# A transformer block on one core: value weights loaded from ScalarE's DMA queue, and the five engine queues rewritten

## The chip, the cores and the metric

The kernel runs on one core of a Trainium2 chip. The metric is the device time of one execution in microseconds (us), the median of several runs. A core has five engines with a queue of instructions each: TensorE (PE in the profile, its weight loads PEld), VectorE (DVE), ScalarE (ACT), GpSimd (POOL) and SyncE (SP), which here only issues DMAs. The DMAs of all queues move their bytes on the core's 16 DMA engines.

## The reference

One block, with x of 2048 rows and D = 448 columns, bf16, 16 heads of Dh = 28 and F = 1792:

```python
def _A_ref(x, wqkv, w_phi, wo):
    qkv = (x @ wqkv).reshape(B, S, 3, H, Dh)            # q, k, v
    pq, pk = einsum("bhsd,hdf->bhsf", q, w_phi), einsum("bhsd,hdf->bhsf", k, w_phi)
    phi_q = concat([softmax(pq), softmax(-pq)]);  phi_k = concat([softmax(pk), softmax(-pk)])
    kv = einsum("bhsf,bhsd->bhfd", phi_k, v);  z = einsum("bhsf->bhf", phi_k)
    num = einsum("bhqf,bhfd->bhqd", phi_q, kv)
    den = einsum("bhqf,bhf->bhq", phi_q, z)[..., None] + 1e-6
    return (num / den) @ wo
def _B_ref(x, w_gate, w_up, w_down):
    return (sigmoid(x @ w_gate) * (x @ w_up)) @ w_down
h  = x + _A_ref(layernorm(x), wqkv, w_phi, wo)
h2 = h + _B_ref(layernorm(h), w_gate, w_up, w_down)
```

Since kv sums over all 2048 rows, no query row can be finished before the last key row has been added.

## The kernel before

The rows are cut into 16 tiles t of 128. Names carry the tile: `pva7` belongs to tile 7. Work runs in stages.

**Head.** SP's queue loads x (`x0`, `x1` are one tile each, `x2`, `x4`, ... two tiles each) and the key and value weights (`ld_k0`, `ld_k2`, `ld_v0`, `ld_v2`), and ACT's queue loads the four small pieces of w_phi (`wphi0` to `wphi3`). Key weights are transposed on PE (`wT0` to `wT3`), copied out of PSUM (`wTe`), multiplied with w_phi (`w2m0_0` to `w2m0_3`) and copied out again (`w2e0_0` to `w2e0_3`): from then on a key projection gives pk directly. Per tile, DVE takes row statistics of x (`bst`, `agg`), POOL or DVE makes the reciprocal root (`ve1`, `pow1`, `nm1`, `nb1`), and one of three engines normalises (`xn`). Tiles 0 to 3 are transposed on PE (`xT`) and copied out (`xTe`); later tiles are transposed by a DMA that SP issues. PE fills its early waits with matmuls on zeros (`warm0`, ...).

**Key/value stage.** Tiles 0 to 3 are projected in pairs of tiles: `ppa`/`ppb` for pk, `vva`/`vvb` for v; later tiles one by one, `pva`/`pvb` doing both. Each a or b part is 8 or 6 matmuls on 64 rows of the array, an upper and a lower half side by side. ACT takes two exponentials of pk (`ek`), DVE sums them by head (`ss`) and inverts the sums (`rs`), POOL or DVE multiplies (`phi`), an engine copies v (`v1`), and PE adds the tile's share of kv (`kva`, `kvb`). The query weights are folded with w_phi in the same way (`ld_q`, `w2m1`, `w2e1`).

**Transition.** The query side (`pqa`, `pqb`, then `eq` on ACT) starts, the sums of kv are masked (`kvz`), and per tile come `num`, the division on DVE (`rsm`, `qq`, `b`, `c`, `den`, `rden`), `o` on POOL or DVE, a transpose (`oT`), the output projection (`woa`, `wob`), the residual (`h`), the second layernorm (`nm`, `sq`, `ve`, `pow2`, `hn`) and its transpose (`hT`).

**Second half.** `ga`, `gb` are gate and up for a group of tiles, `sig` (ACT) and `hh` (DVE) their product; `dn`, `dp`, `dm` the down projection, `fin` the last addition and `out` the store. The `dm` parts use all 128 rows of the array, the others 64 rows.

The program is a graph of such named operations. Their dependencies (and with them the semaphore waits) follow from the tiles that they read and write, but the order in which each engine runs them is written out by hand in `ORDER`, one list of names per engine; where an operation may run on two or three engines, the list that names it decides. An engine runs its list strictly in order, so an operation that waits holds up all that stand behind it. Lines that the prediction names: loads L388, copies out of PSUM L471, statistics L485 and L486, normalisation L511 and L514, paired matmuls L289, fillers L464, `ek` L599 and L600, `ss` L603, `rs` L604, `phi` L607, full-height matmuls L814.

Of the kernel before, what the change touches and what calls it, by code (L numbers as in the profile page):

```python
# [18 lines left out]
class Graph:  # L19
# [86 lines left out]
    def emit(self, nc):  # L106
# [114 lines left out]
    "pe": (
        "warm0 wT1 wT0 warm1 xT1 warm2 xT0 warm3 wT2 wT3 w2m0_0 warm4 w2m0_1 w2m0_3 w2m0_2 warm5 xT2 warm6 ppa0 warm7 "
        "ppb0 xT3 vva0 vvb0 ppa2 ppb2 vva2 vvb2 kva0 w2m1_1 w2m1_0 kvb0 kva1 pva4 kvb1 pvb4 w2m1_3 w2m1_2 pva5 pva6 "
        "pvb5 pvb6 kva2 pqa0_0 kvb2 pva7 kva3 pvb7 pva8 kvb3 pvb8 pva9 kva4 pvb9 kvb4 pva10 kva5 pvb10 pva11 kvb5 "
        "kva6 pvb11 kvb6 pva12 kva7 pvb12 pva13 kvb7 pvb13 kva8 pva14 kvb8 kva9 pvb14 kvb9 pqb0_0 kva10 pva15 kvb10 "
        "kva11 pvb15 kvb11 kva12 pqa0_1 kvb12 kva13 pqb0_1 kvb13 kva14 pqa1_0 kvb14 kva15 kvb15 pqb1_0 pqa1_1 num0 "
        "num1 pqb1_1 pqa2_0 pqb2_0 num2 pqa2_1 oT0 pqb2_1 oT1 num3 woa0 wob0 pqa3_0 num4 pqb3_0 pqa3_1 pqb3_1 num5 "
        "hT0 hT1 ga0_1 gb0_1 ga0_0 num6 gb0_0 ga0_3 woa2 gb0_3 ga0_2 wob2 gb0_2 num7 ga0_5 gb0_5 ga0_4 gb0_4 ga0_7 "
        "gb0_7 ga0_6 num8 gb0_6 woa4 ga0_9 ga0_8 gb0_9 gb0_8 wob4 ga0_11 ga0_10 gb0_11 gb0_10 woa6 num9 wob6 ga0_13 "
        "ga0_12 gb0_13 gb0_12 dn0_0 dn0_4 ga2_0 ga2_1 gb2_0 gb2_1 dn0_8 dn0_11 ga2_3 num10 ga2_2 gb2_3 dp0_0 gb2_2 "  # L230
        "dp0_4 ga2_5 ga2_4 gb2_5 gb2_4 dp0_8 dp0_11 ga2_6 ga2_7 gb2_6 gb2_7 woa8 ga2_8 ga2_9 gb2_8 gb2_9 wob8 num11 "
        "ga2_10 ga2_11 gb2_10 gb2_11 dn2_0 ga2_12 ga2_13 gb2_12 gb2_13 dn2_4 dn2_8 ga4_1 num12 gb4_1 ga4_0 dn2_11 "
        "gb4_0 dp2_0 ga4_3 ga4_2 gb4_3 dp2_4 num13 gb4_2 ga4_5 dp2_8 gb4_5 ga4_4 dp2_11 gb4_4 ga4_7 num14 gb4_7 ga4_6 "
        "woa10 gb4_6 ga4_9 wob10 gb4_9 ga4_8 num15 gb4_8 ga4_11 woa12 gb4_11 ga4_10 wob12 gb4_10 ga4_13 dn4_0 ga4_12 "
        "gb4_13 gb4_12 dn4_4 ga8_1 ga8_0 gb8_1 gb8_0 dn4_8 dn4_11 ga8_3 ga8_2 dp4_0 gb8_2 dp4_4 dp4_8 gb8_3 ga8_4 "
        "dp4_11 gb8_4 ga8_5 woa14 gb8_5 ga8_6 wob14 gb8_6 ga8_7 dn6_0 gb8_7 dn6_4 ga8_8 ga8_9 dn6_8 gb8_9 gb8_8 "
        "dn10_0 dn6_11 ga8_11 ga8_10 gb8_11 gb8_10 dp6_0 dp6_4 dp6_8 ga8_13 ga8_12 gb8_13 gb8_12 dp6_11 dn10_4 dn10_8 "
        "ga12_0 ga12_1 gb12_0 dn8_0 dn10_11 gb12_1 ga12_2 dp10_0 ga12_3 dn8_4 gb12_3 gb12_2 dp10_4 dn8_8 ga12_5 "
        "dn8_11 ga12_4 gb12_5 gb12_4 dp8_0 dp8_4 ga12_7 ga12_6 gb12_7 dp10_8 dp10_11 gb12_6 dp8_8 dp8_11 ga12_9 "
        "ga12_8 gb12_9 gb12_8 dm14_0 dm12_0 dm15_0 ga12_11 ga12_10 gb12_11 gb12_10 dm12_4 dm14_4 dm13_0 ga12_12 "  # L240
        "ga12_13 gb12_12 gb12_13 dm15_4 dm14_8 dm15_8 dm12_8 dm15_10 dm14_10 dm14_12 dm14_13 dm15_12 dm12_10 dm12_12 "
        "dm15_13 dm12_13 dm13_4 dm13_8 dm13_10 dm13_12 dm13_13 "
    ),
# [62 lines left out]
def build(nc, A_x, A_wqkv, A_w_phi, A_wo, B_w_gate, B_w_up, B_w_down, out):  # L306
# [10 lines left out]
    with ExitStack() as es:  # L317
# [570 lines left out]
```

The softmax here doesn't subtract the row's maximum and nothing guards it: scores larger than these inputs give would overflow.

## Time and profile before

| | |
|---|---|
| Median of 8 runs | 208.28 us (208.02 to 208.48) |
| The profiled execution | 208.14 us, span of its instructions 206.4 us |
| PE busy | 198.5 us (96%), 2457 matmuls |
| DVE, ACT, POOL busy | 136.6 (66%), 95.2 (46%), 58.9 us (29%) |
| DMA | 16.25 MB, of these 15.86 MB on queue q1 (SP) and 0.03 MB on q10 (ACT) |
| Chain that ended last | PE 87%, DVE 4%, POOL 3%, DMA 2% |

Busy time is the union of the instructions' spans. PE's matmuls are pipelined and overlap, so a busy PE may still lose time between two starts; how far apart the starts of consecutive operations lie says more. The profiled execution is 1.74 us longer than its span, and 0.14 us below the median.

### The profile page before, as it was taken

The page shows a single profiled execution, that of the slowest core. Times are in us where ns is not written, and L with a number is a line of the kernel's source. Part 1 is how long each engine was busy: PE and PEld are TensorE (multiplying, and loading weights), DVE is VectorE, ACT ScalarE, POOL GpSimd, SP SyncE. Part 2 cuts the span into 40 slices and gives each one's busy share as a digit, 9 for nine tenths or more (in the row PEclk, how much of TensorE's full clock was granted, in tenths as well). Part 3 has the DMA queues.
Part 4 walks back from the last instruction along what each step waited for, and adds up shares of the span by engine and source line. Part 5 has one row for each costly group of instructions (what it writes and reads, how often), then busy time and mean ns, then how long its engine had stood idle before and what let it go on. Part 6 is the DMA issues. An engine that isn't in the chain of part 4 may idle for free.

```text
span 206.4 us, 5794 instructions
## 1 busy us (share of the span) xinstructions
PE 198.5 (96%) x2457; PEld 111.6 (54%) x2457; DVE 136.6 (66%) x343; ACT 95.2 (46%) x185; POOL 58.9 (29%) x99
## 2 busy tenths in 40 slices
PE   7899999999989999999999999999999999999991
PEld 2736666775446666676444444445555545544450
DVE  5999999978899896767768977346332513353151
ACT  2699999879792536222333442334323122122100
POOL 4868999832345404400032020001400000000000
PEclk9999999999999999999999999999999999999999
DMA  6955444899022270414006511130521000020013
GB/s 162 277 117 141 79 93 89 249 380 283 31 51 54 54 183 6 79 29 51 3 0 79 121 29 25 21 35 22 56 71 25 3 0 3 0 89 3 0 38 118
DMA packets 32722, 16.25 MB, mean 79 GB/s; under 512 B 24952, under 2 KB 31800, under 8 KB 32696
## 3 DMA queue, kind: packets, MB, share of 16 engines
q1 hardware_dynamic: 32192, 15.86, 32.5%
q8 instruction: 19, 0.31, 0.7%
q10 hardware_dynamic: 504, 0.03, 0.2%
q14 instruction: 7, 0.06, 0.1%
HBM read 8.34 MB, written 1.84 MB: 49 GB/s over the span
## 4 chain that ended last, share of the span: by engine, by line
PE 87%; DVE 4%; POOL 3%; DMA 2%; issue 1%; ACT 1%; SPq 1%
PE psum L289 80%; PE psum L814 5%; DMA x_sb<-in_A_x_dram 2%; POOL o_pad L700 1%; PE psum L478 1%; POOL rst L728 1%; SPq L388 1%; DVE hn_pad L732 1%; DVE st L485 1%; ACT eq L637 0%; PE psum L553 0%; ACT eq L638 0%; POOL xn_pad L514 0%; PE psum L464 0%; DVE hhT L788 0%
## 5 line engine op out<-in xcount | busy, mean ns | idle before, releaser
L289 PE MATMUL psum<-xnT,wg_sb 64*128 64x512 bf16 (+1 forms) x490 | 94.6, 334 | 0.7 <-DVE qq L685 0.6
L289 PE MATMUL psum<-xnT,wu_sb 64*128 64x512 bf16 (+1 forms) x490 | 94.5, 334 | 0.3
L787 ACT ACTIVATE sg_sb<-psum 128x512 bf16<-128x512 f32 (+1 forms) x70 | 35.0, 511 | 89.9 <-PE psum L289 89.4
L788 DVE SCALAR_TENSOR_TENSOR hhT<-sg_sb,psum 128x512 bf16<-128x512 bf16 (+1 forms) x70 | 39.1, 575 | 50.8 <-ACT sg_sb L787 50.3
L289 PEld LDWEIGHTS psum<-xnT,wg_sb 64*128 64x128 bf16 x490 | 43.9, 94 | 23.9 <-DVE hhT L788 4.8
L289 PEld LDWEIGHTS psum<-xnT,wu_sb 64*128 64x128 bf16 x490 | 43.8, 94 | 15.2 <-PE psum L289 1.4
L289 PE MATMUL psum<-wd_sb,hhT 64*128 64x448 bf16 x336 | 37.1, 349 | 0.0
L289 PEld LDWEIGHTS psum<-wd_sb,hhT 64*128 64x128 bf16 x336 | 17.0, 94 | 15.0 <-DVE x_sb L718 0.6
L607 POOL TENSOR_TENSOR phi<-hhT,rs 128x896 bf16<-128x896 bf16 x13 | 22.7, 1767 | 2.6 <-DVE rs L604 1.5
L289 PE MATMUL psum<-wv_sb,xnT 64*128 64x448 bf16 x112 | 22.0, 350 | 0.1
L289 PE MATMUL psum<-Wk,xnT 64*128 64x448 bf16 x112 | 22.0, 350 | 0.1
L726 POOL TENSOR_SCALAR ve<-ssq 128x1 f32<-128x1 f32 x16 | 3.0, 190 | 61.2 <-ACT junk L723 60.5
L603 DVE TENSOR_REDUCE ss<-hhT 128x32 f32<-128x896 bf16 x16 | 17.0, 1070 | 1.1 <-ACT hhT L600 1.0
L700 POOL TENSOR_TENSOR o_pad<-c_sb,rden 128x448 bf16<-128x448 bf16 x12 | 11.2, 935 | 19.0 <-DVE rden L695 17.4
L289 PE MATMUL psum<-xnT,Wq 64*120 64x512 bf16 x112 | 14.7, 381 | 0.2
L289 PE MATMUL psum<-wo_e,oT 64*128 64x448 bf16 x56 | 13.2, 350 | 0.2 <-DVE oT L471 0.2
L289 PE MATMUL psum<-wo_o,oT 64*128 64x448 bf16 x56 | 13.2, 350 | 0.1
L289 PEld LDWEIGHTS psum<-v,phi 64*120 64x120 bf16 x256 | 10.9, 131 | 3.3 <-PE psum L289 0.2
L821 DVE SCALAR_TENSOR_TENSOR x_sb<-psum,x_sb 128x448 bf16<-128x448 f32 x16 | 9.4, 620 | 3.5 <-PE psum L814 3.1
L723 ACT ACTIVATE junk<-x_sb,nm 128x448 bf16<-128x448 bf16 x16 | 10.6, 663 | 2.2 <-DVE nm L721 2.1
L289 PE MATMUL psum<-v,phi 64*120 64x116 bf16 x256 | 11.1, 213 | 0.1
L814 PE MATMUL psum<-wd_sb,hhT 128*128 128x448 bf16 x56 | 11.1, 353 | 0.0
(82 smaller groups left out, 238.5 us busy)
## 6 DMA issues: line engine op xcount, KB each, us to landing
out_dram<-x_sb SPq DMA_DIRECT2D x16, 112.0 KB, 1.8
x_sb<-in_A_x_dram SPq DMA_DIRECT2D x7, 224.0 KB, 4.2
wd_sb<-in_B_w_down_dram SPq DMA_DIRECT2D x7, 224.0 KB, 3.9
wg_sb<-in_B_w_gate_dram SPq DMA_DIRECT2D x3, 448.0 KB, 6.2
wu_sb<-in_B_w_up_dram SPq DMA_DIRECT2D x3, 448.0 KB, 8.2
wv_sb<-in_A_wqkv_dram SPq DMA_DIRECT2D x2, 224.0 KB, 5.0
wk_sb<-in_A_wqkv_dram SPq DMA_DIRECT2D x2, 196.0 KB, 3.4
wo_e<-in_A_wo_dram SPq DMA_DIRECT2D x1, 336.0 KB, 3.3
```

Of the source, the lines that this page charges most:

```text
L289: p = e.matmul(o, lhsT=w, rhs=r, start=st, stop=sp, tile_position=(row, 0))
L388: return op(eng, name, lambda e: e.dma_start(dst, src), r=r, w=w, dma="in" if eng == "sp" else "ain", nring=48 if eng == "sp" else 8, kb=kb)
L478: p = e.transpose(ps[:, kt * P:(kt + 1) * P], src, ident[:])
L603: op("dve", "ss%d" % t, lambda e: e.tensor_reduce(ss[:, s, :], eks, AX.X, ALU.add), r=[("ek", s)], w=[("ss", s)])
L607: return e.tensor_tensor(phi[:, sp, :, :, :].rearrange("p a g (f n) -> p (a g f) n", f=2)[:, :, 0:56].rearrange("p b (h d) -> p b h d", h= ...
L700: return e.tensor_tensor(o_pad[:, so, off:off + D].rearrange("p (h d) -> p h d", h=H), c_sb[:, s, :, 0:DH], rden[:, s, :][:, :, None].to_b ...
L723: op("act", "sq%d" % t, lambda e: e.activation(junk[:, t % 2, :], h_sb[:, t, :], ACT.Square, bias=nm2[:, t:t + 1], accum_out=ssq2[:, t:t + ...
L726: op("pool", "ve%d" % t, lambda e: e.tensor_scalar(ve2[:, t:t + 1], ssq2[:, t:t + 1], 1.0 / D, EPS, op0=ALU.mult, op1=ALU.add), r=[("ssq2" ...
L787: op("act", "sig" + nm, lambda e: e.activation(sg_sb[:, k, 0:N], bk(bg)[:, 0:N], ACT.Tanh, scale=0.5), r=[B(bg)], w=[("sg", k)])
L788: op("dve", "hh" + nm, lambda e: e.scalar_tensor_tensor(out=hhT[(t0 // 4) % NHH][:, ff, ns], in0=sg_sb[:, k, 0:N], scalar=1.0, in1=bk(bu)[ ...
L814: p = e.matmul(bk(b)[:, 0:D], lhsT=hb[:, ff, TS(t)], rhs=wd_sb[:, ff, :], start=ff == 0, stop=ff == FT - 1)
L821: op("dve", "fin%d" % t, lambda e: e.scalar_tensor_tensor(out=h_sb[:, t, :], in0=bk(b)[:, 0:D], scalar=0.5, in1=h_sb[:, t, :], op0=ALU.mul ...
```

## The change

The two value loads are issued by ACT, behind the w_phi loads; key loads and x stay with SP. The fillers shrink from 9 of 512 columns and 36 of 128 columns to 9 and 16. All five lists in `ORDER` are written anew. In the head, x is loaded as x2, x0, then k2, x1, k0; DVE also normalises tile 0 and copies `w2e0_0`, ACT takes `wTe2`, `xT1e` and `xn2`; the value projection of tiles 0 and 1 starts before the key projection, and its parts alternate with those of the key projection. In the key/value stage some copies and `phi` change engines. Towards the transition, `pqb0_0` moves up beside `pqa0_0`; several weight loads change places. At the end, all `ga12`/`gb12` parts stand before the first `dm` part.

```diff
 ORDER = {
     "sp": (
-        "x1 x0 ld_k0 x2 ld_k2 x4 x6 ld_v0 x10 ld_v2 ld_q2 x8 ld_q3 ld_q1 ld_q0 xT4 xT5 xT6 x14 x12 xT7 ld_woe1 xT8 "
+        "x2 x0 ld_k2 x1 ld_k0 x4 x8 x6 x10 ld_q2 x14 ld_q3 ld_q1 ld_q0 xT4 xT5 xT6 x12 xT7 xT8 xT9 ld_woo1 xT10 xT11 "
+        "ld_wg2 xT12 ld_wd0 xT13 xT14 xT15 ld_wu0 ld_wu3 ld_wd5 ld_wg3 ld_wg1 ld_woe1 ld_wg0 ld_woe0 ld_wu1 ld_wd6 "
+        "ld_woo0 ld_wu2 ld_wd3 ld_wd2 oT3 oT2 ld_wd4 oT5 oT4 oT6 ld_wd1 oT7 hT2 hT3 oT8 oT9 hT5 hT4 hT6 hT7 oT10 oT11 "
...
     "act": (
-        "wphi3 wphi2 wphi1 wphi0 wTe1 wTe0 wTe3 w2e0_0 w2e0_1 w2e0_2 w2e0_3 xn3 xn4 ek0 ek1 xn5 v1_0 v1_1 xn6 ek2 ek3 "
+        "wphi0 wphi1 wphi3 wphi2 ld_v2 ld_v0 wTe2 wTe3 wTe1 wTe0 w2e0_2 xT1e w2e0_1 w2e0_3 xn2 xn3 v1_0 ek0 ek1 xn6 "
+        "ek2 v1_2 v1_3 ek3 w2e1_0 w2e1_1 ek4 v1_4 w2e1_2 w2e1_3 ek5 v1_5 xn10 v1_6 ek6 xn11 ek7 xn12 ek8 v1_8 xn13 "
+        "ek9 v1_9 xn14 ek10 xn15 ek11 ek12 v1_12 ek13 eq0_0 ek14 ek15 v1_15 v1_14 eq0_1 eq1_0 eq1_1 oT0e eq2_1 eq2_0 "
...
     "pe": (
-        "warm0 wT1 wT0 warm1 xT1 warm2 xT0 warm3 wT2 wT3 w2m0_0 warm4 w2m0_1 w2m0_3 w2m0_2 warm5 xT2 warm6 ppa0 warm7 "
-        "ppb0 xT3 vva0 vvb0 ppa2 ppb2 vva2 vvb2 kva0 w2m1_1 w2m1_0 kvb0 kva1 pva4 kvb1 pvb4 w2m1_3 w2m1_2 pva5 pva6 "
+        "warm0 wT2 wT3 warm1 wT1 wT0 warm2 xT0 warm3 w2m0_2 warm4 xT1 w2m0_1 w2m0_3 w2m0_0 warm5 vva0 ppa0 vvb0 ppb0 "
+        "xT3 xT2 vva2 ppa2 ppb2 w2m1_0 vvb2 kva0 w2m1_1 kvb0 pva4 kva1 pvb4 kvb1 pva5 w2m1_2 w2m1_3 pvb5 pva6 pqa0_0 "
...
     "dve": (
-        "zero bd0 bst1 agg1 bst0 agg0 ve1_0 nm1_0 nm1_1 xn1 bst2 bst3 agg2 agg3 ve1_3 xT0e wTe2 bst5 nm1_3 bst4 agg5 "
-        "agg4 bst6 xT1e ve1_4 bst7 agg7 agg6 bst10 xT2e bst11 agg10 xT3e nm1_6 ss0 agg11 rs0 ss1 bst8 rs1 bst9 agg8 "
+        "zero bd0 bst2 bst0 bst3 agg0 agg3 ve1_0 bst1 nm1_0 agg1 ve1_1 xn0 agg2 bst5 xn1 ve1_3 bst4 xT0e agg5 bst8 "
+        "agg4 w2e0_0 bst6 bst7 agg8 bst10 v1_1 agg7 agg6 ve1_6 xT3e xT2e ss0 rs0 ss1 agg10 rs1 bst11 bst9 ss2 agg9 "
...
     "pool": (
-        "ident0 phipad wqpad mask0 neghalf ident ve1_1 pow1_1 pow1_0 xn0 v1ones mask1 nm1_2 ve1_2 pow1_2 nb1_2 xn2 "
+        "phipad mask0 neghalf ident0 ident pow1_0 v1ones nm1_1 pow1_1 nm1_2 ve1_2 pow1_2 pow1_3 mask1 nm1_3 ve1_4 "
...
         def kload(a, b):
             load("ld_k%d" % a, wk_sb[:, a:b, :], A_wqkv[a * GP:b * GP, D:2 * D].rearrange("(kt p) n -> p kt n", p=GP),
-                 [("wk", kt) for kt in range(a, b)], (b - a) * 98)
+                 [("wk", kt) for kt in range(a, b)], (b - a) * 98, eng='sp')
 
         def vload(k):
             r0 = ROW0[k]
             load("ld_v%d" % k, wv_sb[:, k:k + 2, :], A_wqkv[r0:r0 + 256, 2 * D:3 * D].rearrange("(kt p) n -> p kt n", p=P),
-                 [("wv", k), ("wv", k + 1)], 224)
+                 [("wv", k), ("wv", k + 1)], 224, eng='act')
...
-        for i, (n, size) in enumerate(((9, 512), (1, 128), (5, 128), (1, 128), (8, 128), (9, 128), (9, 128), (3, 128))):
+        for i, (n, size) in enumerate(((9, 512), (5, 128), (2, 128), (1, 128), (4, 128), (4, 128))):
             op("pe", "warm%d" % i, warm(n, size), r=["zero"], w=[B(3)])
```

## The prediction

> **What bounds the kernel now.** I read the page first, then the busy time by stretches, the chain of waits, and in the timeline the few instructions on which the head hangs.
>
> ```profile
> PE 198.5 (96%) x2457; PEld 111.6 (54%) x2457; DVE 136.6 (66%) x343; ACT 95.2 (46%) x185; POOL 58.9 (29%) x99
> ```
>
> PE looks like the only bound. The stretches show where others stand beside it (columns: PE, PEld, DVE, ACT, POOL busy us, granted clock, DMA share, GB/s):
>
> ```profile
> 8.00:10.00 2.00, 1.81 (x33) 1.64 (x33) 2.00 (x8) 1.55 (x4) 1.73 (x5) 1.00 1.14 226
> 10.00:12.00 2.00, 2.00 (x23) 0.78 (x20) 1.97 (x8) 1.48 (x2) 1.77 (x8) 1.00 0.99 236
> 20.00:30.00 10.00, 10.00 (x144) 6.20 (x142) 9.96 (x23) 9.57 (x20) 9.62 (x13) 1.00 0.49 99
> 30.00:40.00 10.00, 10.00 (x170) 6.95 (x166) 9.45 (x15) 8.93 (x19) 9.44 (x6) 1.00 0.57 137
> ```
>
> Until 12 us the DMA engines are full and DVE has no gap. From 20 to 40 us all four compute engines are full: DVE is as much the bound of the key/value stage as PE. The chain shows the way in:
>
> ```profile
> 2.17 3.46 DMA x_sb<-in_A_x_dram
> ...
> 8.53 0.78 POOL xn_pad L514
> 9.31 0.05 issue
> 9.36 0.40 PE psum L478 x4
> 9.75 0.50 PE psum L464 x9
> 10.26 0.86 PE psum L289 x8
> ```
>
> Landing of x2, its normalisation, xT2, nine fillers, then the first projection ppa0. From there PE runs almost without holes. In the timeline, the first `ek` and the first and last links of DVE's stage (start, duration):
>
> ```profile
> 12.11 0.54 ACT L599 ACTIVATE hhT<-psum 128x448 bf16<-128x448 f32 x1
> 13.12 1.09 DVE L603 TENSOR_REDUCE ss<-hhT 128x32 f32<-128x896 bf16 x1 [0.19 <-ACT hhT L600]
> ...
> 43.76 1.09 DVE L607 TENSOR_TENSOR phi<-hhT,rs 128x896 bf16<-128x896 bf16 x1
> ```
>
> ss0 starts at 13.12, phi15 ends at 44.85, kva15 starts at 44.94: that is the stage, 31.7 us on DVE. The end of the chain:
>
> ```profile
> 184.83 2.38 PE psum L814 x12
> 187.20 3.13 PE psum L289 x28
> 190.33 2.38 PE psum L814 x12
> 192.71 3.13 PE psum L289 x28
> 195.84 6.17 PE psum L814 x32
> ```
>
> PE changes five times between 64-row and full-height parts.
>
> **The loads.** Landings in the trace, in order of issue: x1 2.86, x0 3.35, k0 4.78, x2 5.62, k2 6.43, x4 7.75, x6 8.36, v0 9.02, x10 9.58, v2 10.23. That is 112, 224, 420, 644, 840, 1064, 1288, 1512, 1736, 1960 KB in sum. Each load lands some 4 to 5 us after issue, though SP issues one in 0.47 us: bytes set the pace, not issuing. So the 2 x 0.43 us of issuing that leave SP buy nothing by themselves; on ACT they push its table load (3.40, 1.28 us) to about 4.3, ended by 5.6, when wT2 is just done: at most 0.1 us.
>
> In the new order 840 KB (x2, x0, k2, x1, k0) still come before x4: x2 at 3.35, x0 at about 4.2, x1 at 5.6 (644 KB), k0 at 6.4 to 6.8. On ACT's queue v stands behind w_phi, whose pieces landed between 3.69 and 6.62, so v flows from about 5.6 on, beside x4. From which engine a byte is ordered doesn't change the full DMA share of 0.99 to 1.14. Bounds for x4: without v's share fourteen of the sixteen engines had delivered their part by 7.00 and the last by 7.75; eight packets of v (41 ns each in the trace) between those of x4 make 7.3 at the earliest; if all of v went first, 1512 KB make 9.02. I take 7.9, near the old last part plus half of v's packets. v itself is complete with x10, at about 10 (1960 KB: 10.23).
>
> The Trainium skill speaks against this change: "DMA: Bandwidth & Descriptors", section "Rules for kernel authors", says that spreading DMAs over several issuing engines doesn't help bandwidth, since they share 16 engines, and saves only issue time. By that rule x4 would lie at my 7.9 or later; if the queues were independent, at 7.0 or earlier, and the head below would be some 0.7 us shorter.
>
> **Head, step by step** (DVE, start to start: statistics 0.54, `xn` and transposed copies 0.35, small ones 0.09, copy of f32 0.54, from the timeline): bst2 3.4, bst0 4.2, bst3 4.7, agg0, agg3, ve1_0 5.5, bst1 5.65, nm1_0, agg1, ve1_1, xn0 6.6, agg2 6.95, then bst5 stands in the queue and waits for x4: 7.9. Behind it xn1 8.45, ve1_3, bst4 8.9, xT0e 9.4, agg5, bst8 9.85, agg4, w2e0_0 10.5 to 11.1. ACT: wTe's until 7.9, w2e0_2, xT1e 9.4, w2e0_1, w2e0_3 until 10.7. So vva0 starts at about 10.1, ppa0, which needs all four w2e0, at 11.15 (before: 10.19). PE then runs ppa0 0.75, vvb0 0.57, ppb0 0.57 plus its drain: ek0 at 13.25 instead of 12.11. DVE: v1_1 after vvb0 at 12.75, xT3e 13.6, xT2e 13.95, ss0 at 14.3 instead of 13.12: **1.2 us late**.
>
> PE itself loses nothing: an a part followed by its own b part waits for the drain (ppa0 to ppb0 1.13 us instead of 0.75, vva0 to vvb0 0.99), which the alternation with another pair hides. I get pva6 at 22.0 with pvb5 done, against 21.41 + 0.57. The 20 fillers taken away (56 ns each, 1.1 us) stood partly in the way: ppa0 could have begun at 9.75, when w2e0_3 was done, and began at 10.19 behind nine fillers. That 0.4 us is part of the times above; what is late next is w2e0_0.
>
> DVE after ss0 has 16 `ss`, 16 `rs`, 6 statistics and three `phi` in both orders. It gains a v copy (0.55), loses w2e1_0 (0.54) and one of two `xn` (0.4): 0.4 us less. So phi15 ends some 0.8 to 1.2 us later: I take **+1.0**. Bounds: 0, if PE and not DVE decides the stage (then pva6 decides, even); +2, if x4 comes at 8.7 and v at 11. Covered and put at nothing: wg2 between xT11 and xT12 (448 KB, 1.5 us at 300 GB/s, against 2.4 us from xT12's landing at 30.60 to pva12 at 33.05); woo0 later among the loads (by their bytes at about 50.5; woa0 starts at 53.58; each us later than that would show at woa0); ld_wd1 behind oT6 (about 72, dn0_0 at 77.78).
>
> **Transition.** Between 45.4 and 73.2 PE loses 4.2 us against its usual distances, nearly all of it drains of adjacent a and b parts and waits for oT1e, wob0's residual and hT1e, which stand in the same order after. eq2_1 before eq2_0 goes with pqa3_1 before pqa3_0. oT0e now stands before both eq2 on ACT and waits for oT0 (51.94) while ACT idles from 50.43; eq3_0 then ends at 61.55, where ga0_1 needs it at 61.68: covered by 0.1 us only. hn3 moved behind hh0_9 takes away the 0.28 us before ga0_11. Sum **-0.1**; bounds -0.6 and +0.5 (an `eq` of 1.94 us partly uncovered).
>
> **End.** Each change between forms of matmul costs 0.1 us (dm15_0 to ga12_11 0.85 instead of 0.757, and so on); five become one: **-0.4**, bounds -0.5 and 0. Behind the last matmul nothing moves: fin13 and out13 follow it as before, 4.4 us to the end.
>
> Sum against the profiled execution's own 208.14: +1.0 - 0.1 - 0.4 = 208.64. That execution lies 0.14 below the median, so **208.8 us**, 0.25% slower. About 0.2% (0.42 us) is what a measurement can tell from no change.
>
> **Rivals.** *The loads overlap as the order supposes* (faster): x4 lands by 7.2, so bst5 never waits, w2e0_0 ends at about 10.4 and ss0 starts near 13.4. Then DVE's 0.4 us less work makes the stage end where it did, and the transition and end give -0.5 to -0.9: 207.3 to 207.8. For it: fourteen engines had x4 at 7.00. Against it: two had not, and v now comes between. It decides as soon as x4 is under about 7.5. *v queues behind w_phi* (slower still): ACT's queue is strictly in order, w_phi's last piece landed at 6.62, and if x's larger packets (1792 bytes against 896) take most of the turns, v ends near 11 and vva0 starts at 11: one more us, 209.5 to 210.2. *PE's clock falls*: fewer fillers leave PE about half empty between 5 and 10 us. In the trace nine 512-column fillers took 3.84 us, 427 ns each, and later ones run at half that; if PE went back to that pace for 3 us of projections it would cost 1.5 us or more, 210.5 and up. The trace shows no such fall, but it has no gap of that length either.
>
> **Numbers.** My case (208.1 to 209.5) 0.50; the loads overlap 0.28; v late 0.14; clock 0.08. From these: faster 0.31, within 0.2% 0.20, slower 0.49. The range 207.2 to 210.2 takes in the first three with their bounds.
>
> **What would show it.** Right: bst5 starts when x4 lands, after 7.5, with DVE idle before it; w2e0_0 ends near 11; ek0 near 13.2; ss0 near 14.3; kva15 about 1 us later; one change of form at the end. Wrong: ppa0 before 10.5, ss0 before 13.5 (faster), or fillers and projections at 427 ns (clock), or kva15 unmoved although ss0 is late, which would mean that DVE had slack in the stage.

## The result, and the profile after

The changed kernel takes 210.30 us (median of 11 runs, 209.38 to 211.50), the kernel before 208.33 us beside it (31 runs, 207.90 to 209.16). The ratio is 1.0097 with a 95% interval of 1.0082 to 1.0111: 2.0 us slower, where 0.5 us was predicted and the range ended at 210.2. The sign was right, the size was not. The profiled execution of after took 210.62 us, with a span of 208.9 us against 206.4; its lines of code are one number higher than those of before.

In the stretches (columns as before: PE, PEld, DVE, ACT, POOL busy, granted clock, DMA share, GB/s) PE is less busy in the head (1.68 and 1.19 us where it had 1.81 and 2.00) and no longer full in the key/value stage:

```profile
8.00:10.00 2.00, 1.68 (x28) 1.46 (x29) 1.77 (x6) 1.31 (x4) 1.85 (x5) 1.00 1.36 366
10.00:12.00 2.00, 1.19 (x17) 0.75 (x16) 2.00 (x7) 1.78 (x4) 1.61 (x7) 1.00 0.77 128
20.00:30.00 10.00, 10.00 (x142) 6.20 (x140) 9.35 (x25) 9.92 (x21) 9.13 (x13) 1.00 0.52 88
30.00:40.00 10.00, 9.14 (x160) 5.90 (x156) 8.92 (x15) 8.15 (x17) 8.87 (x6) 1.00 1.05 176
```

Two places catch the eye. From 10 to 12 us the DMA engines move 128 GB/s (before: 236) although loads are waited for; and from 30 to 40 us PE stands still for 0.86 us, where before it had no gap (10.00 of 10.00 us). The chain of waits (start, us, what) shows the head and the end:

```profile
3.14 5.07 DMA x_sb<-in_A_x_dram
...
10.25 0.88 ACT Wk L472 x2
11.13 0.13 issue
11.26 2.27 PE psum L290 x22
...
100.98 92.81 PE psum L290 x936
193.79 10.71 PE psum L815 x56
```

x4 lands at 8.21, vva0 starts at 11.26, and at the end one change of matmul form stands where there were five. That the chain names ACT's copy ahead of vva0 is a coincidence: v0 landed at 11.12, the copy w2e0_3 ended at 11.12, and vva0 reads only v and x. In an experiment below with the same head, vva0 starts while that copy still runs.

The waits of PE between 20 and 50 us (total, times, longest) hold one entry, and the timeline has its place, the first matmul of pva13:

```profile
PE psum L290 <- DMA xnT<-xn_pad: 0.8, 1, 0.8
```

```profile
37.77 0.35 PE L290 MATMUL psum<-Wk,xnT 64*128 64x448 bf16 x1 [0.85 <-DMA xnT<-xn_pad]
```

It waits for the transposing DMA xT13, issued at 32.27 and landed at 37.63. Against PE's usual distance between these parts pva13 starts 1.02 us late. The view of the tile that holds the value weights gives the time from issue to landing of its two loads, first of before, then of after:

```profile
DMA to landing us min/median/max: 4.9/5.0/5.1
```

```profile
DMA to landing us min/median/max: 6.7/7.0/7.3
```

The instructions that the prediction watched: first `ek`, `ss0`, `phi15` (start, duration).

```profile
14.12 0.54 ACT L600 ACTIVATE hhT<-psum 128x448 bf16<-128x448 f32 x1
15.18 1.08 DVE L604 TENSOR_REDUCE ss<-hhT 128x32 f32<-128x896 bf16 x1
...
46.30 1.36 DVE L608 TENSOR_TENSOR phi<-hhT,rs 128x896 bf16<-128x896 bf16 x1
```

ss0 is 2.06 us later than before, kva15 (47.71 against 44.94) 2.77 us. Comparing where PE stands with the work already done, after is 1.3 us behind at pva6, 1.5 at pva12, 2.5 at pva13, 2.8 at kva15, 2.9 at ga0_0, and 2.5 at the last matmul. So there are three things to explain: the head, pva13, and 0.3 us at the stage's end; 0.4 us come back at the end. The third is mostly phi15 itself, which kva15 follows at once: it takes 1.36 us, as in all twelve profiles with the new order of this stage (1.36), and 1.09 in the four with the old one. In the new order POOL works on phi14 beside it, in the old one POOL is idle at that time; that this is the reason isn't shown.

### The profile page after: what moved, and what is told of

It reads as the page before. It is cut to its first block, busy times and chain, and to the rows that moved or that the text cites. A ratio compares the mean times of both kernels' runs of the same rounds, so it can differ in the third digit from the quotient of the medians.

```text
span 208.9 us, 5759 instructions
## 1 busy us (share of the span) xinstructions
PE 197.7 (95%) x2437; PEld 110.4 (53%) x2437; DVE 135.5 (65%) x342; ACT 94.8 (45%) x184; POOL 61.7 (30%) x101
## 4 chain that ended last, share of the span: by engine, by line
PE 79%; DVE 6%; DMA 5%; ACT 4%; POOL 2%; issue 1%; SPq 1%; DVEq 0%; POOLq 0%
PE psum L290 73%; PE psum L815 5%; DMA xnT<-xn_pad 3%; DMA x_sb<-in_A_x_dram 2%; ACT hhT L600 1%; SPq L389 1%; DVE ss L604 1%; ACT hhT L601 1%; DVE st L486 1%; ACT xn_pad L512 1%; PE psum L479 1%; ACT v L472 1%; POOL rst L729 1%; DVE xnT L472 1%; POOL rst L499 0%
## 5 line engine op out<-in xcount | busy, mean ns | idle before, releaser
L789 DVE SCALAR_TENSOR_TENSOR hhT<-sg_sb,psum 128x512 bf16<-128x512 bf16 (+1 forms) x70 | 39.7, 577 | 44.9 <-ACT sg_sb L788 44.5
L290 PE MATMUL psum<-wd_sb,hhT 64*128 64x448 bf16 x336 | 38.6, 349 | 0.0
L290 PEld LDWEIGHTS psum<-wd_sb,hhT 64*128 64x128 bf16 x336 | 16.5, 94 | 15.7 <-DVE x_sb L719 0.6
L290 PE MATMUL psum<-wv_sb,xnT 64*128 64x448 bf16 x112 | 22.5, 350 | 1.6 <-ACT Wk L472 0.8
L290 PE MATMUL psum<-Wk,xnT 64*128 64x448 bf16 x112 | 22.5, 349 | 0.9 <-DMA xnT<-xn_pad 0.8
L701 POOL TENSOR_TENSOR o_pad<-c_sb,rden 128x448 bf16<-128x448 bf16 x14 | 13.1, 935 | 33.5 <-DVE rden L696 30.9
L290 PEld LDWEIGHTS psum<-v,phi 64*120 64x120 bf16 x256 | 10.5, 131 | 3.7 <-POOL phi L608 0.4
L486 DVE BATCH_NORM_STATS2 st<-x_sb 128x6 f32<-128x448 bf16 x16 | 9.3, 606 | 3.4 <-DMA x_sb<-in_A_x_dram 3.4
L290 PEld LDWEIGHTS psum<-Wk,xnT 64*128 64x128 bf16 x112 | 8.3, 94 | 5.6 <-issue 1.3
```

The costliest lines, as they stand in the source:

```text
L290: p = e.matmul(o, lhsT=w, rhs=r, start=st, stop=sp, tile_position=(row, 0))
L486: op("dve", "bst%d" % t, lambda e: e.bn_stats(st1[:, t, :], x_sb[:, t, :]), r=[("x", t)], w=[("st1", t)])
L701: return e.tensor_tensor(o_pad[:, so, off:off + D].rearrange("p (h d) -> p h d", h=H), c_sb[:, s, :, 0:DH], rden[:, s, :][:, :, None].to_b ...
L789: op("dve", "hh" + nm, lambda e: e.scalar_tensor_tensor(out=hhT[(t0 // 4) % NHH][:, ff, ns], in0=sg_sb[:, k, 0:N], scalar=1.0, in1=bk(bu)[ ...
```

## Experiments

All ratios are to the kernel before, run beside; brackets are 95% intervals. One point of a percent is 2.1 us.

### The queue of the value loads

`v_on_sp`, against the changed kernel:

```diff
-  sp:  "... ld_k0 x4 x8 x6 x10 ..."            act: "... wphi2 ld_v2 ld_v0 wTe2 ..."
+  sp:  "... ld_k0 x4 ld_v2 ld_v0 x8 x6 x10 ..." act: "... wphi2 wTe2 ..."
-                 [("wv", k), ("wv", k + 1)], 224, eng='act')
+                 [("wv", k), ("wv", k + 1)], 224)
```

> The changed kernel with one thing undone: the two loads of the value weights go back to SyncE's queue, right behind x4; every order is otherwise that of the changed kernel. Theory (v lands late because it stands behind w_phi on ScalarE's queue): v0 lands at about 9.0 to 9.7 us instead of 11.12, vva0 starts at about 10 instead of 11.26 and the head gives back some 0.8 to 1.2 us, so 209.1 to 209.6 us. Rival (bytes decide, the queue does not): v0 lands near 11 all the same, or x4 is late in its place, and the time stays at 210.1 to 210.5.

Measured: 209.54 us, ratio 1.0061 [1.0040, 1.0082]. v0 landed at 8.73, vva0 started at 9.57, and the profiled span fell by 1.2 us to 207.7. By the medians 0.8 us came back. The value tile's loads and vva0 in this run:

```profile
DMA to landing us min/median/max: 4.4/4.5/4.6
```

```profile
9.57 0.93 PE L288 MATMUL psum<-wv_sb,xnT 64*128 64x448 bf16 x8
```

How the loads come late is seen in the landing of a load's sixteen parts (the trace has sixteen marks for each of these loads; us):

```
v0, after    8.64 8.71 9.02 9.24 9.46 9.46 9.49 9.59 9.69 9.79 9.84 9.87 9.96 10.18 10.79 11.12
v0, v_on_sp  8.03 8.04 8.10 8.18 8.18 8.21 8.24 8.27 8.27 8.33 8.39 8.40 8.45  8.61  8.62  8.73
```

On ScalarE's queue, beside x on SyncE's, the parts lie 2.5 us apart; behind x4 in one queue 0.7. But the middle parts are some 1.3 us later too, so the spread is only about half of it. The other half is in the packets of the two queues, here from 8 to 9 us of after (q1 is SyncE's, q10 ScalarE's; packets, MB, share of the DMA engines):

```profile
q1 hardware_dynamic: 148, 0.24, 63.9%
q10 hardware_dynamic: 159, 0.14, 39.5%
```

The queues send about as many packets each, x in packets of 1792 bytes and v in 896, so x8, x6 and x10 take some 60% of the bytes while the head waits for v. In `v_on_sp` v goes ahead of these three.

All seven profiles of new-head kernels with v on ScalarE have v0 at 10.2 to 11.1 (parts 1.2 to 2.5 us apart), all five with v on SyncE at 8.7 to 9.3 (0.6 to 1.2); after's own profile is the latest of the seven. x4 hardly differs: 7.5 to 8.2 against 7.4 to 8.0. Nor does x10, the last of these loads: 10.6 to 11.7 against 10.5 to 11.1. So the bytes together take about as long either way, and what the edit changes is who comes first. It changes the queue and the place in the order at once; v on SyncE's queue behind x10 wasn't tried.

`before_v_act`, against the kernel before:

```diff
-  sp:  "... x4 x6 ld_v0 x10 ld_v2 ld_q2 ..."   act: "... wphi0 wTe1 ..."
+  sp:  "... x4 x6 x10 ld_q2 ..."               act: "... wphi0 ld_v0 ld_v2 wTe1 ..."
-                 [("wv", k), ("wv", k + 1)], 224)
+                 [("wv", k), ("wv", k + 1)], 224, eng='act')
```

> The kernel before with one thing done: the value weights go on ScalarE's queue behind w_phi, every order otherwise as before. Theory (late v costs only where the head wants it early): v lands at about 11, x4 and x6 somewhat sooner, and since vva0 ran at 12.33 anyway the time is that of before, 208.0 to 208.6. Rival (the queue itself costs, by pushing ScalarE's table load or by crowding x): +0.5 to +1.2, 208.8 to 209.5.

Measured: 209.06 us, ratio 1.0026 [1.0000, 1.0052], between the two, and with a wide scatter (208.06 to 211.18). The profiled execution was the slowest of them: the last part of x4 landed at 9.43, the fifteenth at 7.91, and with it bst5, xT1e and ppa0 were 1.7 us late. So the second queue can hurt x as well, in this one execution at least. Its 3.0 us aren't all x4's, though: PE waited 1.78 us for ppa0, and then its granted clock fell to half from 12.04 to 15.45 us (the column ahead of the last two numbers):

```profile
12.00:14.00 2.00, 2.00 (x13) 0.74 (x11) 1.97 (x7) 1.11 (x2) 1.77 (x7) 0.51 0.86 195
```

### Loads between transposing DMAs

`loads_late`, against the changed kernel:

```diff
-  sp: "... xT10 xT11 ld_wg2 xT12 ld_wd0 xT13 xT14 xT15 ld_wu0 ..."
+  sp: "... xT10 xT11 xT12 xT13 xT14 xT15 ld_wg2 ld_wd0 ld_wu0 ..."
```

> The changed kernel with ld_wg2 and ld_wd0 moved from between the transposes xT11, xT12 and xT13 to behind xT15. Theory (xT13 is held up by the load ahead of it): xT13 lands some 2.5 us after its issue instead of 5.36, the matmuls pva13 lose nothing instead of 1.02 us, and 0.7 to 1.0 us come back: 209.3 to 209.6. Rival (DVE's chain of the stage, not xT13, decides when the stage ends): pva13 does not wait, but kva14 and kva15 wait longer for it, and the time is 210.0 to 210.4.

Measured: 210.17 us, ratio 1.0089 [1.0067, 1.0112]. pva13 lost nothing, as the theory says, yet the time didn't follow, and not for the rival's reason: counted from vva0, kva15 gained the full 1.0 us. The next place gave it back. The other loads were now behind wg2 and wd0, woo0 landed at 54.99, and woa0 lost 1.08 us where it had lost 0.36:

```profile
55.34 0.35 PE L288 MATMUL psum<-wo_e,oT 64*128 64x448 bf16 x1 [0.91 <-DVE qq L684]
```

The releaser named is an engine long done; woo0's landing is what came last. In the same run PE waited for v itself, which settles the coincidence of the first section (vva0 started at 10.52, w2e0_3 ended at 10.54):

```profile
PE psum L288 <- DMA wv_sb<-in_A_wqkv_dram: 0.7, 1, 0.7
```

`v_sp_loads` undoes both and puts woo0 behind them; against `v_on_sp`:

```diff
-  sp: "... xT11 ld_wg2 xT12 ld_wd0 xT13 xT14 xT15 ld_wu0 ... ld_wd6 ld_woo0 ld_wu2 ..."
+  sp: "... xT11 xT12 xT13 xT14 xT15 ld_wg2 ld_wd0 ld_woo0 ld_wu0 ... ld_wd6 ld_wu2 ..."
```

> The changed kernel with both suspected losses undone: the value weights on SyncE's queue behind x4, and ld_wg2, ld_wd0 and also ld_woo0 issued in a row behind xT15 (ld_woo0 so that woa0 doesn't wait for it). Theory (v's landing and xT13 carry the whole difference, and they add up): vva0 near 9.6 us, no wait at pva13 and none above 0.4 us at woa0; the profiled span is 208.9 - 1.2 - 1.0 = 206.7, a time of 208.1 to 208.6, level with the kernel before. Rival (DVE's chain bounds the key/value stage, as the prediction had it): pva13 is free but kva14 and kva15 wait some 0.5 us or more, and the time is 208.9 to 209.5.

Measured: 208.76 us, ratio 1.0024 [1.0004, 1.0043]; span 206.8. No wait at pva13, none above 0.36 at woa0; 0.16 us over the expected range, and the rival's longer waits are absent: kvb14 and kvb15 lose 0.23 and 0.27 us, just as in the changed kernel. PE is full again from 30 to 40 us:

```profile
30.00:40.00 10.00, 10.00 (x176) 6.73 (x174) 9.60 (x17) 9.16 (x17) 10.00 (x6) 1.00 0.65 147
```

These two repairs take 1.5 of the 2.0 us away, about half each (1.0097 to 1.0061 to 1.0024; each step is uncertain by some 0.3 points).

`before_wg_wd` puts the same two loads between the transposes of the kernel before:

```diff
-  sp: "... xT11 xT12 xT13 xT14 ld_woo1 xT15 ld_wd0 ... ld_wg0 ld_wg2 ..."
+  sp: "... xT11 ld_wg2 xT12 ld_wd0 xT13 xT14 ld_woo1 xT15 ... ld_wg0 ..."
```

> The kernel before with one thing done: ld_wg2 moved to between xT11 and xT12, ld_wd0 to between xT12 and xT13. Theory (a load between transposes of the same queue makes the next transpose late, whatever the head did): xT13 lands some 5 us after its issue instead of 3.28, at 35.5 to 37, pva13 (34.61 before) starts 1 us or more later, and the time is 209.0 to 209.8. Rival (the 2.4 us that the prediction counted cover it): 208.2 to 208.6.

Measured: 210.16 us, ratio 1.0080 [1.0052, 1.0107]. The two loads cost 1.6 us there, with the old head. xT12 landed at 34.96 and xT13 at 36.72, so the wait fell on pva12 already:

```profile
35.10 0.35 PE L289 MATMUL psum<-Wk,xnT 64*128 64x448 bf16 x1 [1.43 <-DMA xnT<-xn_pad]
```

Three more runs tried to tell which property of the loads does it. `wd0_late` moves only ld_wd0 behind xT15; `small_load` exchanges ld_wd0 (224 KB) with ld_woe1 (56 KB); `loads_on_act` issues both loads from ScalarE (their `eng` argument changes with the lists):

```diff
-  sp: "... xT11 ld_wg2 xT12 ld_wd0 xT13 xT14 xT15 ld_wu0 ... ld_wg1 ld_woe1 ld_wg0 ..."
+  sp: "... xT11 ld_wg2 xT12 xT13 xT14 xT15 ld_wd0 ld_wu0 ... ld_wg1 ld_woe1 ld_wg0 ..."     (wd0_late)
+  sp: "... xT11 ld_wg2 xT12 ld_woe1 xT13 xT14 xT15 ld_wu0 ... ld_wg1 ld_wd0 ld_wg0 ..."     (small_load)
+  sp: "... xT11 xT12 xT13 xT14 xT15 ld_wu0 ... ld_wg1 ld_woe1 ld_wg0 ..."                   (loads_on_act)
-  act: "... xn12 ek8 v1_8 xn13 ek9 ..."
+  act: "... xn12 ld_wg2 ek8 v1_8 xn13 ld_wd0 ek9 ..."                                       (loads_on_act)
```

> The changed kernel with ld_wd0 alone moved from between xT12 and xT13 to behind xT15; ld_wg2 stays between xT11 and xT12. Theory A (each load holds up the transpose directly behind it): xT12 lands as late as before the move (about 34.4 us), xT13 about 3.3 to 3.9 us after its issue at 32.27 instead of 5.36, pva13 (due at 36.75) loses nothing, and the whole 1.0 us comes back without the wait at woa0: 209.2 to 209.5. Theory B (wg2 with its 448 KB is what blocks): xT13 still lands after 37, pva13 still loses 0.8 us or more, 210.0 to 210.5.

> The changed kernel with the places of ld_wd0 (224 KB) and ld_woe1 (56 KB) exchanged, so that a quarter of the bytes stands between xT12 and xT13. Theory A (the bytes of the load hold up the transpose): 168 KB less at some 300 GB/s are 0.55 us, so pva13 still loses about 0.5 us and the time is 209.7 to 210.0. Theory B (any load between two transposes costs, whatever its size): xT13 lands after 37 as before, 210.1 to 210.5. Theory C (the packets of the load on sixteen engines, not its bytes, and the small one is gone at once): pva13 loses nothing, 209.2 to 209.5.

> The changed kernel with ld_wg2 and ld_wd0 issued from ScalarE at the same time as before (behind xn12 and xn13), so that the same bytes move in the same microseconds but don't stand between transposes in SyncE's queue. Theory A (standing in the transposes' own queue is what delays xT13): xT13 lands about 2.5 us after its issue, pva13 does not wait, 209.2 to 209.6. Theory B (the bytes and the shared engines delay it, from whichever queue): xT13 still takes 4 us or more, pva13 waits as it did, 210.0 to 210.6.

Measured: 210.60, 210.27 and 210.95 us, ratios 1.0096 [1.0075, 1.0116], 1.0086 [1.0066, 1.0106], 1.0110 [1.0081, 1.0138]: no gain in any. Without wd0, pva13 was free but pva12 lost 1.00 us, since xT12 landed at 35.46 (34.41 in after). With the small load pva12 lost 0.90 (xT12 35.04). So wd0 isn't needed, wg2 is enough, and neither theory of `wd0_late` nor one of `small_load` had the wait move forward. From ScalarE's queue it is no better: in the profiled execution, the slowest of its six, xT11 took 5.96 us, xT12 7.63 us, and PE lost 2.4 us at pva11 and pva12; by the medians it can't be told from the changed kernel. So it isn't the place in the queue of the transposes: plain loads that run beside transposes are enough.

### The instruction load

In each of these traces one packet of 16 KB of instructions (queue q8), which takes 0.9 to 2.0 us, falls into the flight of xT12 or xT13: at 30.54 in before, 33.80 in after, 32.81 in `wd0_late`, 32.88 in `before_wg_wd`. Up to 45 us such packets come every 8 to 11 us. Wherever the loads stand in SyncE's queue between the transposes, one of them is close by. What the loads do without it shows in `loads_on_act`: xT11 landed at 34.95, ahead of the instruction load at 35.49 (only one of 8 KB, at 32.83, was in its flight), and pva11 lost 0.9 of the 2.4 us. Two kernels moved the instruction loads, by 28 narrow matmuls on zeros ahead of vva2, where PE waits anyway; `fetch_shift` is `v_sp_loads` with them, `fetch_after` the changed kernel:

```diff
+        def narrow(e):
+            for _ in range(28):
+                p = e.matmul(bk(4)[0:32, 0:32], lhsT=zero[:, 0:32], rhs=zero[:, 0:32], start=True, stop=True)
+            return p
+        op("pe", "narrow", narrow, r=["zero"], w=[B(4)])
-  pe: "... xT3 xT2 vva2 ppa2 ..."
+  pe: "... xT3 xT2 narrow vva2 ppa2 ..."
```

> The run with v on SyncE's queue and the three loads behind xT15, with 28 narrow matmuls (32 columns) more on PE in the gap ahead of vva2, where PE waits for xT2e anyway. They take about 0.7 us of that gap and move the instruction loads of 16 KB, which come after so many PE instructions, about 2 us earlier: the third one from 31.73 to about 29.6 us. In that run xT12 landed 2.4 us after its issue and xT13, with the instruction load inside its flight, 3.9 us. Theory A (the instruction load holds up the transpose in flight): xT13 takes about 2.5 us and xT11 or xT12 takes 3 us or more instead. Theory B (the transposes are late by what they queue behind, the instruction load does nothing): xT13 takes 3.9 us again and xT12 2.4. The time is 208.6 to 209.0 in both.

Measured: 209.31 us, ratio 1.0037 [1.0015, 1.0059]. The third instruction load didn't move as expected: it came at 32.69, as far behind pva6 as before, again into xT13's flight (3.4 us; xT12 2.4). The second one did move against the transposes: from 22.91, inside xT8's flight, to 22.48, inside xT7's, while xT7 and xT8 themselves were issued 1.1 us later. The lateness went along: xT7 from 2.4 to 4.2 us, xT8 from 3.8 to 2.4. Fifteen parts of xT7 landed by 22.95, the sixteenth at 24.66. In the stretches between, next to nothing starts (the view counts a packet where it starts, the instruction load at 22.48 in the first row):

```profile
22.00:22.50 0.50, 0.50 (x11) 0.31 (x8) 0.40 (x1) 0.50 (x3) 0.50 (x3) 1.00 0.83 172
22.50:23.00 0.50, 0.50 (x10) 0.31 (x8) 0.48 (x1) 0.50 (x2) 0.50 (x2) 1.00 0.00 0
23.00:23.50 0.50, 0.50 (x10) 0.23 (x6) 0.50 (x1) 0.50 (x2) 0.50 (x1) 1.00 0.01 1
23.50:24.00 0.50, 0.50 (x8) 0.29 (x6) 0.50 (x3) 0.50 (x3) 0.50 (x2) 1.00 0.00 0
24.00:24.50 0.50, 0.50 (x8) 0.31 (x6) 0.50 (x2) 0.50 (x3) 0.50 (x1) 1.00 0.62 124
```

The instruction load ended at 23.39, and the next packet of 256 bytes, the size that the transposes move, starts at 23.37. Nothing of xT8 landed before that sixteenth part. That one part waits for the DMA engine with the instruction load is an inference from these times: the trace doesn't name the DMA engine of a packet.

> The changed kernel with the same 28 narrow matmuls ahead of vva2, so that the third instruction load moves from 33.8 to about 31.7 us, into the flight of wg2 instead of those of wd0 and xT13. Theory A (load between transposes and instruction load add up, one behind the other): the wait moves from pva13 (1.02 us) to pva12, since xT12 lands near 35 to 36; the sum of both waits stays at 0.7 to 1.3 us and the time at 209.9 to 210.5. Theory B (the loads alone do it): pva13 waits 1 us as before.

Measured: 209.62 us, ratio 1.0059 [1.0032, 1.0085], faster than expected and some 0.7 us faster than the changed kernel itself, by 28 matmuls that compute nothing. The instruction load came at 31.88, 15 parts of xT12 at 32.38 to 32.54 and the sixteenth at 34.89, then wd0 at 35.36 and xT13 at 35.99. The wait moved from pva13 to pva12 and shrank to 0.59 us:

```profile
35.02 0.35 PE L288 MATMUL psum<-Wk,xnT 64*128 64x448 bf16 x1 [0.42 <-DMA xnT<-xn_pad]
```

So the place is theory A's: load and instruction load come one behind the other, and which transposes they hit is a matter of a microsecond. Its size isn't: the wait is 0.59 where 0.7 to 1.3 was expected, and the time is below its range.

### The two halves, and the copy in the head

`second_half` is the kernel before with the changed orders from num0, eq0_1, kvz0 and o0 on; `first_half` is the opposite. On PE, against the kernel before and against the changed kernel:

```diff
-  pe: "... kvb15 pqb1_0 pqa1_1" + "num0 ..." of the kernel before
+  pe: "... kvb15 pqb1_0 pqa1_1" + "num0 ..." of the changed kernel        (second_half)
-  pe: "... kvb15 pqb1_0 pqa1_1" + "num0 ..." of the changed kernel
+  pe: "... kvb15 pqb1_0 pqa1_1" + "num0 ..." of the kernel before         (first_half)
```

> The kernel before as far as the end of the key/value stage, and the changed kernel's order from num0, eq0_1, kvz0 and o0 on. Theory (the new order of the transition is worth about nothing, the end 0.4 us): 207.8 to 208.1, with one change between forms of matmul at the end instead of five. Rival (the transition costs, since oT0e stands ahead of both eq2 and the cover is 0.1 us): the end's gain is used up, 208.3 to 208.8.

> The changed kernel as far as the end of the key/value stage, and the order of the kernel before from num0, eq0_1, kvz1 and o0 on. Theory (the halves add up: the second half of the change is worth 0.4 us): 210.5 to 210.9, 0.2 to 0.5 us above the changed kernel. Rival (the second half's gain exists only behind the early stage of before): level with the changed kernel, 210.1 to 210.4, or below it.

Measured: 208.14 us, ratio 0.9981 [0.9967, 0.9995], and 210.84 us, ratio 1.0111 [1.0090, 1.0131]. The first is 0.4 us faster than the kernel before and so the best of all; its chain ends with one change of form:

```profile
98.08 92.81 PE psum L288 x936
190.89 10.71 PE psum L813 x56
```

The second differs from the changed kernel by 0.3 us in the expected direction, less than its interval can tell.

`best` is `v_sp_loads` with the copy that ppa0 waits for moved up on DVE, `best2` the same with agg4 ahead of it:

```diff
-  dve: "... xT0e agg5 bst8 agg4 w2e0_0 bst6 ..."
+  dve: "... xT0e agg5 w2e0_0 bst8 agg4 bst6 ..."     (best)
+  dve: "... xT0e agg5 agg4 w2e0_0 bst8 bst6 ..."     (best2)
```

> As the run with v on SyncE's queue and the three loads behind xT15, and w2e0_0 two places earlier on DVE (ahead of bst8 instead of behind agg4), since ppa0 waits for it. Theory (ppa0 is bound by w2e0_0 alone, then by w2e0_3 at about 10.3): ppa0 starts at about 10.4 instead of 10.73, ss0 0.3 to 0.4 us sooner, 207.8 to 208.2. Rival (the head's gain is taken up by the stage, which is bound by the transposes and statistics behind bst8): 208.2 to 208.6, the same as without it.

> As the run named best, but with agg4 kept ahead of w2e0_0 on DVE (agg5, agg4, w2e0_0, bst8). Theory (in best it was agg4, behind bst8, that held POOL's ve1_4 at 10.98, with it nb1_2, xn2, xn3 and v1_0 in front of ek0): xn2 starts by 10.9 instead of 11.39, ek0 by 13.2 instead of 13.67, and the time is 208.4 to 208.8, no worse than without the moved w2e0_0. Rival (the copy ahead of bst8 costs by itself, since bst8 and its followers are late): 209.3 to 210.0 as in best.

Measured: 209.87 us, ratio 1.0058 [1.0036, 1.0080], and 208.80 us, 1.0029 [1.0007, 1.0051]. In `best` ppa0 did come sooner (10.50 against 10.92) and ek0 later (13.67 against 13.13). agg4, now behind bst8, held POOL's next step, and ACT's xn2 and xn3, ahead of ek0, waited for POOL. In the timeline:

```profile
10.98 0.23 POOL L492 TENSOR_SCALAR ve<-mv 128x2 f32<-128x2 f32 x1 [0.65 <-DVE mv L485]
```

```profile
11.39 0.81 ACT L510 ACTIVATE xn_pad<-x_sb,nb,rst 128x512 bf16<-128x512 bf16 x1 [0.95 <-POOL nb L501]
```

With agg4 back in front the time is that of `v_sp_loads`, but the moved copy itself gained nothing. In the profiled execution of `best2` x4 landed 0.4 us later than in `v_sp_loads`, and ek0 was no sooner, so its expected instants were not met there.

## Why the prediction was wrong, and where it was right

**Loads: half right, and the first failed step.** x4 was put at 7.9 and landed at 8.21; k0 at 6.4 to 6.8, landed 6.98; x1 at 5.6, landed 6.54. v was put "at about 10" by the sum of bytes. That holds for its first load (v2 10.06), not for v0 (11.12). The sum itself was wrong: it let v be complete with x10 at 1960 KB, but x8 now stands ahead of x10, which makes 840 + 4 x 224 + 448 = 2184 KB. At the pace of before, from 644 KB at 5.62 to 1960 KB at 10.23, that is about 11.0, near what the seven profiles show (v0 10.2 to 11.1, x10 10.6 to 11.7). The step reasoned besides that the issuing engine doesn't matter, because the DMA engines are full either way. The bytes did flow (366 GB/s from 8 to 10 us, against 226 before), but two queues share them by packets, so the wanted v comes in with x8, x6 and x10 instead of ahead of them, and a load is there only when its last sixteenth is, which came up to 2.5 us behind its first.

The prediction weighed the rule of the Trainium skill, "DMA: Bandwidth & Descriptors", section "Rules for kernel authors", that spreading DMAs over issuing engines doesn't help, since they interleave on the same 16 engines. The runs agree (x10 lands about as late either way) and go further: the value loads took 7.0 us from issue to landing on the second queue and 4.5 us in line behind x4.

**Head: the rival's numbers.** w2e0_0 ended at 11.28 (11.1 predicted). But vva0 started at 11.26 instead of 10.1, so ppa0 at 12.01 instead of 11.15, ek0 at 14.12 instead of 13.25, ss0 at 15.18 instead of 14.3, pva6 at 23.30 instead of 22.0. "PE itself loses nothing" fell with v. From ppa0 to pva6 it then took 11.29 us, where the step has 10.85; `v_on_sp` and `v_sp_loads` have 11.29 too, so these 0.4 us aren't v's. (The 1.13 us from ppa0 to ppb0 that the step puts down to the drain hold three fillers, the 0.99 from vva0 to vvb0 none.)

The rival *v queues behind w_phi* had the head: v near 11, vva0 at 11, 209.5 to 210.2. It had 14 in 100. Of its two reasons one holds: x's larger packets do take most of the bytes. The other doesn't: v's first sixteenths landed as early on ScalarE's queue (v2 from 7.16) as on SyncE's (from 7.37), so w_phi in front isn't what made it late. That its time came close to 210.3 is luck, since 0.8 us of that come from the loads between the transposes, which it didn't have.

**Key/value stage: right where it could be tested.** The step took +1.0 for a DVE chain that begins 1.2 us late. In `v_sp_loads`, without the two other losses, ss0 began 1.02 us late (14.14), phi15 ended 0.7 us late (45.54) and kva15 started 0.7 us late. So a late start does reach the stage's end, and the term was some 0.3 us large. Inside it two errors work against each other: phi15 started only 0.43 us late, so the chain made up 0.6 us and not 0.4, and phi15 then took 0.27 us longer than before, which "three `phi` in both orders" didn't foresee.

**"Covered and put at nothing": the other failed step.** It set 448 KB at 300 GB/s, 1.5 us, against 2.4 us of slack at pva12. In after the DMAs of this queue landed strictly one behind the other: xT11 31.14, wg2 33.97, xT12 34.41, wd0 36.99, xT13 37.63. wg2 took 2.8 us from the landing ahead of it, wd0 2.6, of which the instruction load from 33.80 to 35.47 is a part. Together that is 6.5 us from xT11 to xT13, where before it was 3.3. So the mis-sized term is the load's own 1.5 us, which were 2.8, and the second load and the instruction load behind it weren't in the sum at all. The price by the runs is 0.8 us in this kernel (`v_on_sp` to `v_sp_loads`) and 1.6 us in the kernel before (`before_wg_wd`). What the step left out could be read in the trace of before: there, too, the transposes with a 16 KB instruction load early in their flight took longer (xT8 3.4 us, xT13 3.3, against 2.5 of xT9 and xT10). xT11 took 3.2 without one; a packet of 8 KB (queue q14) came in its flight. The step's remark on woo0 was right, though it landed later than its bytes made it (53.16, not 50.5): in after it was covered (woa0 56.39), and in `loads_late`, 1.8 us later, it showed at woa0 at once.

The Trainium skill, "Runtime: NRT & Kernel Launch", section "Instruction fetch mechanics", says that an engine's instructions are fetched by DMA in blocks of 16 KiB and that crossing such a boundary is mostly hidden. The size agrees (19 packets, 0.31 MB on queue q8). It is hidden from PE (busy for 10.00 of 10.00 us from 20 to 30 us of after, with an instruction load at 24.02); it isn't hidden from a DMA transpose in flight, whose last part came 1.7 and 2.4 us after the others in the two runs above.

**Transition and end: right in sum.** -0.1 and -0.4 were predicted; `second_half` gives 0.4 us less for both together, within -0.7 and -0.1.

**The clock: rare, but real.** The prediction gave it 8 in 100, and the profiled execution of after shows full clock from 5.5 us on. Single executions do show it. In the profile of `loads_on_act` PE ran at half clock from 8.0 to 11.4 us:

```profile
8.00:10.00 2.00, 2.00 (x24) 2.00 (x23) 2.00 (x9) 1.16 (x3) 1.85 (x5) 0.50 1.07 362
```

A mean granted clock of 0.992 or less was seen in 19 of 102 executions of kernels with the new head (25 fillers), in none of 79 of the kernel before beside them (45 fillers; lowest 0.994). But one of the 30 executions of the other kernels with 45 fillers shows it too, `before_v_act` above, where PE waited for ppa0: fillers make it rarer and don't rule it out. In `v_sp_loads` the two such executions took 209.7 and 210.1 us against a median of 208.7 of the others; in after, where v comes late anyway, they are no slower. So it doesn't explain the medians. The prediction's price of 1.5 us or more is about what these two executions show (1.0 and 1.5 us).

**The sum as it should have been**, by the ratios: 0.8 us for v's queue, 0.8 us for the loads between the transposes, and 0.5 us that `v_sp_loads` still lies above the kernel before, which is the later stage less the 0.4 us of the end. That makes 2.0 us. That the last 0.5 us equal the predicted difference is partly chance: the stage's 0.7 and the end's -0.4 make 0.3.

## What to carry to other kernels

A load counts when its last sixteenth has landed: moving a wanted load to a second queue, beside others, doesn't bring it sooner by the bytes and may bring it later, by the sharing and by the spread, so keep what the head waits for in one queue in the order of need. When you sum bytes up to a load, count every load that now stands ahead of it. Keep plain loads out of the stretch in which transposing DMAs feed the bottleneck, and give such transposes slack for an instruction load in flight. When a wait disappears and the time stays, look for the next due time behind it: twice here it moved to the neighbour (pva13 to pva12, pva13 to woa0).

## What was not expected of the hardware

- With a 16 KB instruction load in the flight of a DMA transpose, one of its sixteen parts came 1.7 to 2.4 us late in five flights (`fetch_shift`, `fetch_after`, `before_v_act` twice, `before_wg_wd`), and what stands behind in the queue waited meanwhile (0 to 1 GB/s for 1.5 us in `fetch_shift`). In others all parts came late together (xT8 in after 4.0 us, its parts within 0.3 us).
- A plain load directly ahead of a DMA transpose landed all at once: x10 in after with all sixteen parts within 0.08 us at 11.7, v2 in before within 0.08 us at 10.2, while the head's loads with another plain load behind them in the queue land part by part over 0.6 us or more. It isn't a rule: in `before_v_act` x10 has four parts at 8.9 to 9.2 and twelve at 11.2 to 11.6, and woo1, directly ahead of xT10, lands over 1.6 us in `loads_late`.
- 28 matmuls that compute nothing made the changed kernel some 0.7 us faster (1.0097 to 1.0059), by moving an instruction load by 1.9 us. That the whole gain comes from this isn't shown: v also landed 0.75 us sooner in the profiled execution.
- In the profile of `fetch_shift` PE worked at half pace until about 10 us (fillers of 128 columns 106 ns apart instead of 55) although the column of the granted clock says 1.00 there; its stage ran 1.1 us later than that of `v_sp_loads`. The trace's first record of the clock is at 10.20 us there and at 4.42 in `v_sp_loads`, and the column prints 1.00 where it has no record: the full clock came late. The pace of known matmuls says more than the column, and the mean clocks above miss this case.
